# A fused state-read attention and top-2-of-4 mixture of experts: batch 5 in the dense form of batches 6 and 7, with new tables of the order

## The chip, the core and the metric

The kernel runs on one core of a Trainium2 chip, as one program with one launch. The metric is the device time of one execution in microseconds. The engines are TensorE (PE, matrix products; its weight loads are listed apart as PEld), VectorE (DVE), ScalarE (ACT), GpSimd (POOL) and SyncE (SP, which issues the DMAs here). Each engine works through its own list of instructions in order, and semaphores hold an instruction back until what it reads is there.

## What is computed

The first stage reads, per batch and head, a small state with attention in both directions. Its two results are joined, laid out as 544 tokens of 512 numbers per batch, and go through four attention experts, of which each token uses the two with the largest gate. Cut to what matters:

```python
# x (8, 8, 512, 64), state (8, 8, 32, 64): batch, head, token, width
a     = softmax(x @ state.T / 8)            # 512 x 32 per head
xread = a @ state
a2    = softmax(state @ x.T / 8)            # 32 x 512 per head
sread = a2 @ x
y = concat([xread, sread], axis=2)          # 544 tokens per head
y = y.transpose(0, 2, 1, 3).reshape(8, 544, 512)
logits = y @ w_gate                         # 4 experts, the largest 2 count
for e in range(4):
    q, k, v = y @ wq[e], y @ wk[e], y @ wv[e]            # 544 x 64 each
    att = softmax(causal(q @ k.T / 8))
    out += gate weight of e (0 if not chosen) * (att @ v @ wo[e])
```

wq and wk are scaled by 200, so the scores are large. The kernel therefore keeps every fp32 factor as a pair of fp16 numbers (a high half and the rest, the low half) and forms three products of each pair: high by high, high by low, low by high.

## The kernel before

**Work of a batch.** `front(b)` (from L557) loads x, splits it into halves `xh`, turns them into `xT`, forms the first scores and their softmax (`eb`, `mb`, `sbm`; its turned halves are `at`), multiplies the state by the weights (`gs`), and from `at` and `gs` gets the values `v`, the gate, the keys `kt` and the queries `qm`. For each of the four tiles of 128 tokens, `probs(b, unit)` (L920) forms the scores from `kt` and `qm`, adds the causal mask and takes the row maximum `mx` (a custom instruction on DVE), takes the exponential (ACT, tile `p`), splits it into halves `ph`, and turns these with one transposing DMA into `pt`. `reads(b, i)` (L964) multiplies `pt` by `v`, divides by the sum (`su`) and applies the gate (`c`), which gives `z`; its halves `zh` go through another transposing DMA. `result` (L1022) multiplies `z` by `wo_n` and writes the output `o`. `side(b, ...)` and `tail(g)` do the same for the 32 state rows of each batch, two batches at a time.

**Two forms.** A string of one letter per batch (`U` in `CFG`, L19) says how `units_of(b)` (L498) cuts the probabilities. Form S works with two slots: a slot is a query that is zero outside the expert that the token has chosen, so that two experts share one matmul of 128 rows. For it `front` forms Q token by token (24 matmuls of 256 columns), multiplies it by a mask (`qf`, mask `m`), splits it into `qh` and turns it by two transposing DMAs into `qm`. A read has 194 columns, for each of two slots. Form D ("dense") computes all four experts for all tokens, each with 64 rows, two side by side on the upper and lower half of the array. Q comes turned out of the product already (12 matmuls of 512 columns), with no mask and no DMA, and the gate is applied after the read, which has 65 columns for each of four experts. Its units are tile 1; the first two experts of tiles 0 and 2; their other two; and tile 3 in two halves:

```python
"S": [((0, "s"), (1, "s")), ((2, "s"),), ((3, "s"),)],
"D": [((1, "d"),), ((0, "0"), (2, "0")), ((0, "1"), (2, "1")), ((3, "0"),), ((3, "1"),)]
```

`all_experts(b)` (L506) names the tiles that are read densely, and `reads` and `front` branch on it.

**What sets the order.** Nothing is issued where it is written. Class `Steps` (L146 on) records each step with its engine or engines, what it reads and writes, and its buffers. `run` (L256) then plays three packed tables of numbers, `ORDER`: in which order the steps are issued, on which of the possible engines each goes, and which of the rotating buffers each gets. Every instruction is issued in one line there, L266, which is why the profile shows that line alone, and groups are told apart by their tiles:

```python
steps, ways, slots = (zlib.decompress(base64.b85decode(x)) for x in order)
...
for n in memoryview(steps).cast("H"):
    s = self.all[n]
    for f, kw in s["ways"][ways[n]][2]:
        f(**{k: v.ap() if isinstance(v, View) else v for k, v in kw.items()})
```

There are 2 buffers for `ph`, 3 for `pt`, 3 for `p`, and 8 banks of PSUM.

## Time and profile before

| | before |
|---|---|
| median of 3 runs | 278.22 us (277.75 to 279.74) |
| the profiled execution | 278.5 us, its span 276.7 us |
| granted TensorE clock | 1.00 |
| busy, share of the span: PE | 267.8 us, 97% |
| weight loads (beside PE) | 181.4 us, 66% |
| DVE | 248.6 us, 90% |
| ACT | 228.8 us, 83% |
| POOL | 173.9 us, 63% |
| chain that ended last | PE 71%, DVE 14%, ACT 7% |

The span is the time from the first to the last instruction of the profiled execution, and 1.8 us of its time lie around it. Busy shares are means over the whole span. What counts for a change is the stretch in which it lies and what is waited for there. A group of instructions of one form is shown with its count, its total busy time (overlaps counted once) and the mean length of one. Where matmuls overlap, the busy time over the count is less than the mean length, and it is what one of them costs.

### The profile page before, as it was taken

Reading aid. Unit: us, or ns where it says so; the run is one execution under the profiler, and the core shown is the slowest. Engines: PE = TensorE matmul, PEld = TensorE weight load, DVE = VectorE, ACT = ScalarE, POOL = GpSimd, SP = SyncE. Lnnn points to the kernel's source line nnn. Section 1 sums busy time; section 2 is a strip of 40 time slices with the busy share of each in tenths; the row PEclk is TensorE's granted clock in tenths of the full one; section 3 lists DMA queues with packets and bytes.
Section 4 is the critical chain, followed back from the end, with each engine's and each line's share of the span. In section 5 each row is a group of like instructions: output and inputs, shape, how many; then the busy total and the mean of one; then the engine's idle time right before and its main releaser. Section 6 shows DMA issues by size and latency. Waiting matters only on the chain.

```text
span 276.7 us, 9066 instructions
## 1 busy us (share of the span) xinstructions
PE 267.8 (97%) x3392; PEld 181.4 (66%) x3393; DVE 248.6 (90%) x743; ACT 228.8 (83%) x629; POOL 173.9 (63%) x250
## 2 busy tenths in 40 slices
PE   8989999899999999999999999999999999999995
PEld 4856756576477675666776757577477745486663
DVE  1699999999999999999999999998889989999862
ACT  4699999899899998998979888879668898778442
POOL 8852868497974898289859956687684661324000
PEclk9999999999999999999999999999999999999999
DMA  6985699999796999999999899996787988899994
GB/s 188 246 194 119 174 179 222 221 183 188 161 226 136 184 193 238 204 197 192 224 195 246 184 249 164 199 190 167 208 116 139 188 168 191 208 203 168 249 231 152
DMA packets 161804, 53.16 MB, mean 192 GB/s; under 512 B 140640, under 2 KB 157280, under 8 KB 161760
## 3 DMA queue, kind: packets, MB, share of 16 engines
q1 hardware_dynamic: 161760, 52.59, 95.1%
q8 instruction: 26, 0.43, 0.7%
q14 instruction: 18, 0.15, 0.2%
HBM read 11.02 MB, written 8.91 MB: 72 GB/s over the span
## 4 chain that ended last, share of the span: by engine, by line
PE 71%; DVE 14%; ACT 7%; issue 3%; POOL 2%; DMA 1%; DVEq 0%; POOLq 0%; ACTq 0%
PE bank L266 71%; DVE eb L266 2%; ACT p L266 2%; DVE sbm L266 1%; DVE qf L266 1%; DMA a2t<-a 1%; DVE xh L266 1%; DVE p L266 1%; ACT gs L266 1%; DVE gs L266 1%; DVE mb L266 1%; POOL eb L266 1%; ACT v L266 1%; ACT wn L266 1%; DVE m L266 1%
## 5 line engine op out<-in xcount | busy, mean ns | idle before, releaser
L266 PE MATMUL bank<-gs,at 128*128 128x260 f16 (+3 forms) x320 | 43.6, 284 | 0.7 <-ACT gs L266 0.7
L266 ACT ACTIVATE p<-p,mx 128x256 f32<-128x256 f32 (+3 forms) x80 | 41.8, 560 | 2.7 <-POOL mx L266 2.0
L266 PE MATMUL bank<-v,pt 128*128 128x194 f16 (+1 forms) x600 | 41.9, 226 | 0.5 <-DVE qf L266 0.4
L266 PE MATMUL bank<-kt,qm 64*128 64x128 f16 (+7 forms) x384 | 42.2, 299 | 0.0
L266 PEld LDWEIGHTS <-pt 128*128 128x128 f16 x600 | 38.7, 98 | 4.3 <-issue 1.3
L266 DVE CUSTOM_DVE_ANT_0 p<-bank,band 128x384 f32<-128x384 f32 (+3 forms) x80 | 35.9, 480 | 1.6 <-PE bank L266 1.3
L266 PEld LDWEIGHTS <-qm 64*128 64x128 f16 (+1 forms) x384 | 20.8, 95 | 18.4 <-issue 9.3
L266 PEld LDWEIGHTS <-at 128*128 128x128 f16 x288 | 27.7, 97 | 7.4 <-issue 1.1
L266 PE MATMUL bank<-at,gs 128*128 128x512 f16 (+1 forms) x116 | 29.9, 394 | 0.5 <-POOL at L266 0.5
L266 POOL TENSOR_TENSOR ph<-p,ph 128x1024 f16<-128x1024 f32 (+1 forms) x15 | 28.6, 1910 | 2.6 <-DVE ph L266 1.3
L266 PE MATMUL bank<-wo_n,z 128*128 128x512 f16 (+1 forms) x114 | 26.1, 368 | 0.0
L266 DVE SCALAR_TENSOR_TENSOR xh<-xn,xh 128x512 f16<-128x512 f32 x28 | 19.8, 723 | 1.7 <-POOL xh L266 1.5
L266 PE MATMUL bank<-wo_n,zp 128*128 128x512 f16 x84 | 20.3, 379 | 0.1
L266 ACT ACTIVATE o<-bank 128x512 f32<-128x512 f32 (+1 forms) x31 | 17.9, 582 | 2.9 <-PE bank L266 2.8
L266 ACT ACTIVATE z<-bank,c 128x64 f32<-128x64 f32 x78 | 17.4, 323 | 3.0 <-POOL c L266 2.8
L266 ACT ACTIVATE v<-bank 128x256 f16<-128x256 f32 x40 | 15.4, 394 | 3.9 <-PE bank L266 1.9
L266 PEld LDWEIGHTS <-z 128*128 128x128 f16 x114 | 10.7, 99 | 10.5 <-issue 0.9
L266 PEld LDWEIGHTS <-gs 128*128 128x128 f16 x108 | 10.3, 98 | 10.9 <-issue 0.9
L266 POOL TENSOR_TENSOR c<-su,wgt 128x6 f32<-128x6 f32 (+1 forms) x23 | 5.3, 235 | 17.8 <-DVE su L266 15.1
L266 ACT ACTIVATE ph<-p 128x768 f16<-128x768 f32 (+1 forms) x17 | 16.0, 944 | 0.2
L266 PEld LDWEIGHTS <-xh 128*128 128x128 f16 x416 | 14.1, 98 | 3.1 <-POOL xh L266 1.3
L266 POOL TENSOR_TENSOR qh<-qf,qh 128x768 f16<-128x768 f32 x8 | 14.3, 1786 | 2.6 <-ACT qh L266 2.0
(244 smaller groups left out, 674.9 us busy)
## 6 DMA issues: line engine op xcount, KB each, us to landing
out_dram<-o SPq DMA_DIRECT2D x33, 256.0 KB, 2.9
xn<-in_x_dram SPq DMA_DIRECT2D x14, 512.0 KB, 4.8
xn<-in_x_dram SPq DMA_DIRECT2D x4, 256.0 KB, 3.6
...
pt<-ph SPq DMA_TRANSPOSE x28, 4.1
...
```

Source lines behind the costliest of these rows:

```text
L266: f(**{k: v.ap() if isinstance(v, View) else v for k, v in kw.items()})
```

## The change

Batch 5 gets form D in place of form S, and the three tables are replaced by others that fit the new list of steps. The line of `CFG` and the first line of each table:

```diff
-           ... n_tpt=1, n_tz=1, n_pt=3, U="SSSSSSDD")
+           ... n_tpt=1, n_tz=1, n_pt=3, U="SSSSSDDD")
 ORDER = (
-        "c-jrs1A7o^7y!`M-@;nUTD7&cY;SGVP(v--wr$(CZQHhO+jjT<hx0rK0D*u(AQNPU2uKV?peSU4K*$Z=px_H7AtCrcHb@VikOPuJ2zWsl_(29J"
+        "c-jru1A7o^7y!`M-@@7!mR75^wQO#=p`n&-+qP}nwr$(CZM%Da#d(f5!~=r(V1OXt18E>3tOb9_3ArH&6ag<t3l4HXK1c)^pb)Hs^{@dvAt|H)"
...
```

The table is one line shorter, so that the line of all instructions is L265 in the changed kernel. In counts, batch 5 loses 24 matmuls of Q with 256 columns, 60 reads of 194 columns, and its masked queries with two DMAs; it gets 12 matmuls of Q with 512 columns and 120 reads of 65 columns, 8 more masked passes and as many more exponentials, and 20 transposes of 16 blocks for P in the whole kernel where there were 16 (10 of 12 blocks where there were 12). PE has 6493 rows in place of 6397, DVE 739 in place of 734.

The tables also move steps of other batches. From here on the rows are those of the two orders, with the numbers of tiles that tell buffers apart.

On PE, before, batch 5's first scores (those of tiles 0 and 1 together) follow 18 reads of batch 4, and begin with the form of 128 rows:

```order
L266 LDWEIGHTS pt_160
L266 MATMUL bank_84<-v_0_107,pt_160 128x194
L266 LDWEIGHTS qm_136
L266 MATMUL bank_82<-kt_137,qm_136 128x128
L266 LDWEIGHTS qm_136
L266 MATMUL bank_77<-kt_137,qm_136 128x128
L266 LDWEIGHTS qm_136
L266 MATMUL bank_82<-kt_137,qm_136 128x256
```

In the changed order, batch 5's first scores are those of tile 1 alone, 12 matmuls of 256 columns in the form of 64 rows, ahead of value products (`at`, `gs`):

```order
L265 MATMUL bank_83<-tv_0_110,tpt_202 64x259
L265 LDWEIGHTS qm_135
L265 MATMUL bank_80<-kt_139,qm_135 128x256
L265 LDWEIGHTS qm_135
L265 MATMUL bank_84<-kt_139,qm_135 128x256
...
L265 LDWEIGHTS at_122
L265 MATMUL bank_79<-gs_123,at_122 128x260
```

Where a dense read used to come only with batch 6, the first one (65 columns) now stands some 130 matmuls behind these scores, after the tail's products (`wn`, `xt_tail`) and six reads of 194 columns of batch 4:

```order
L265 LDWEIGHTS xt_tail_155
L265 MATMUL bank_82<-wn_75,xt_tail_155 64x132
L265 LDWEIGHTS pt_160
L265 MATMUL bank_84<-v_0_107,pt_160 128x194
...
L265 LDWEIGHTS pt_159
L265 MATMUL bank_83<-v_0_108,pt_159 128x65
```

On SP, which issues all transposes, before, the queries of batch 5 (`qm`) stand between batch 4's P and the outputs, and P of batch 5 comes in transposes of 12 and 16 blocks:

```order
L266 DMA_TRANSPOSE pt_160<-ph_157 128x12x128
L266 DMA_TRANSPOSE qm_136<-qh_142 128x12x128
L266 DMA_TRANSPOSE qm_136<-qh_143 128x12x128
L266 DMA out_dram<-o_179 128x512
L266 DMA_TRANSPOSE a2t_153<-a_0_154 128x8x128
L266 DMA_TRANSPOSE z_184<-zh_186 128x4x128
```

Changed, the two rows of `qm` are gone, and transposes of 16 blocks follow each other with outputs, a transpose of `z` and one of the state path (`a2t`) between them:

```order
L265 DMA_TRANSPOSE a2t_153<-a_0_154 128x8x128
L265 DMA_TRANSPOSE pt_160<-ph_158 128x16x128
L265 DMA out_dram<-o_180 128x512
L265 DMA_TRANSPOSE z_183<-zh_186 128x4x128
L265 DMA out_dram<-o_182 128x512
L265 DMA_TRANSPOSE a2t_153<-a_0_154 128x8x128
L265 DMA_TRANSPOSE pt_161<-ph_157 128x16x128
```

On DVE, at the program's start, before, two passes over the halves of x (`xh`) stand ahead of the first maximum of the softmax (`mb`):

```order
L266 TENSOR_SCALAR xh_95<-xn_87 128x512
L266 SCALAR_TENSOR_TENSOR xh_95<-xn_87,xh_95 128x512
L266 TENSOR_SCALAR xT_97<-bank_80 128x512
L266 TENSOR_REDUCE mb_118<-bank_84 128x16
L266 TENSOR_TENSOR eb_117<-bank_84,mb_118 128x512
```

Changed, there are four of them, and a second copy of `xT`:

```order
L265 TENSOR_SCALAR xT_97<-bank_80 128x512
L265 SCALAR_TENSOR_TENSOR xh_95<-xn_87,xh_95 128x512
L265 TENSOR_SCALAR xh_95<-xn_87 128x512
L265 SCALAR_TENSOR_TENSOR xh_95<-xn_87,xh_95 128x512
L265 SCALAR_TENSOR_TENSOR xh_94<-xn_90,xh_94 128x512
L265 TENSOR_SCALAR xT_97<-bank_82 128x512
L265 TENSOR_REDUCE mb_118<-bank_78 128x16
```

The first maximum has moved behind one more copy of `xT` and two more passes of `xh`.

## Rows read from the trace of the kernel before

**Rows 1.** Busy time by stretch: stretch, length, busy (instructions), clock, DMA share, GB/s.
```profile
40.00:60.00 20.00, 18.67 (x215) 12.30 (x214) 19.09 (x55) 18.92 (x54) 14.12 (x19) 1.00 1.01 198
...
180.00:240.00 60.00, 59.71 (x735) 38.52 (x732) 54.73 (x178) 48.13 (x132) 36.60 (x47) 1.00 0.86 176
```

**Rows 2.** Chain that ended last, three pieces: start us, length us, what.
```profile
120.84 85.44 PE bank L266 x1050
...
208.05 1.72 ACT p L266 x4
...
218.13 55.44 PE bank L266 x662
```

**Rows 3.** PE by form, scores: output<-inputs, shape, count, busy us, mean ns, idle before.
```profile
L266 PE MATMUL bank<-kt,qm 128*128 128x512 f16 x36 | 8.8, 380 | 0.0
...
L266 PE MATMUL bank<-kt,qm 64*128 64x512 f16 x60 | 8.3, 379 | 0.0
L266 PE MATMUL bank<-kt,qm 64*128 64x384 f16 x60 | 7.0, 325 | 0.0
L266 PE MATMUL bank<-kt,qm 128*128 128x384 f16 x36 | 6.9, 327 | 0.0
...
L266 PE MATMUL bank<-kt,qm 128*128 128x256 f16 x36 | 6.2, 273 | 0.0
...
L266 PE MATMUL bank<-kt,qm 64*128 64x128 f16 x60 | 6.0, 216 | 0.0
...
L266 PE MATMUL bank<-kt,qm 64*128 64x256 f16 x60 | 5.5, 272 | 0.0
L266 PE MATMUL bank<-kt,qm 128*128 128x128 f16 x36 | 5.0, 220 | 0.0
```

**Rows 4.** PE by form: reads, Q's two forms, and a product of the state path.
```profile
L266 PE MATMUL bank<-v,pt 128*128 128x194 f16 x360 | 33.4, 247 | 0.5 <-DVE qf L266 0.4
L266 PE MATMUL bank<-at,gs 128*128 128x512 f16 x108 | 26.1, 379 | 0.5 <-POOL at L266 0.5
...
L266 PE MATMUL bank<-gs,at 128*128 128x256 f16 x120 | 14.4, 272 | 0.7 <-ACT gs L266 0.7
...
L266 PE MATMUL bank<-v,pt 128*128 128x65 f16 x240 | 8.5, 194 | 0.0
...
L266 PE MATMUL bank<-wn,bd 64*32 64x512 f16 x168 | 5.9, 379 | 0.0
```

**Rows 5.** Timeline of PE: start us, length us, what, count.
```profile
222.28 0.88 PE L266 MATMUL bank<-wn,xt_tail 128*64 128x128 f16 x24
...
235.89 0.92 PE L266 MATMUL bank<-kt,qm 64*128 64x512 f16 x6
...
239.56 2.76 PE L266 MATMUL bank<-wo_n,zp 128*128 128x512 f16 x12
242.16 1.56 PE L266 MATMUL bank<-xt_tail,wn 128*128 128x64 f16 x48
...
244.22 1.63 PE L266 MATMUL bank<-v,pt 128*128 128x65 f16 x48
```

**Rows 6.** Timeline of SP's queue: the transpose of the probabilities of those scores.
```profile
242.09 1.58 SPq L266 DMA_TRANSPOSE pt<-ph  x1
```

**Rows 7.** Last lines of the views of tiles pt and zh, in this order.
```profile
DMA to landing us min/median/max: 3.2/4.1/6.5
...
DMA to landing us min/median/max: 2.4/3.4/5.7
```

**Rows 8.** The page's costliest groups: masked passes on DVE; POOL by form: low halves.
```profile
L266 DVE CUSTOM_DVE_ANT_0 p<-bank,band 128x384 f32<-128x384 f32 (+3 forms) x80 | 35.9, 480 | 1.6 <-PE bank L266 1.3
...
L266 POOL TENSOR_TENSOR ph<-p,ph 128x1024 f16<-128x1024 f32 x8 | 17.0, 2130 | 1.5 <-DVE ph L266 1.3 <-ACT ph L266 0.2
```

**Rows 9.** Tile xh: DVE's low halves, ns min/median/max, first and last start.
```profile
L266 DVE SCALAR_TENSOR_TENSOR xh<-xn,xh x28: 623/682/1642, 6.7 to 170.1; 128x512 f16<-128x512 f32 x28
```

**Rows 10.** The page's costliest groups: weight loads of the reads.
```profile
L266 PEld LDWEIGHTS <-pt 128*128 128x128 f16 x600 | 38.7, 98 | 4.3 <-issue 1.3
```

More of the change, by code (lines that the diff above doesn't have):

```diff
@@ L20 @@
            FRONT=1.5, FSPAN=1.0, TSPAN=1.3, TOFF=1.2, KT=3, p32=3, ph=2, at=1, et=1, gs=1, xh=4, a2=1, o=4, sn=1, qf=2,
[L21 removed]
+           n_eb=1, n_e2=1, n_a2t=1, n_xt_tail=2, n_z32=3, n_z=2, n_zh=2, n_tq=1, n_tv=2, n_tpt=1, n_tz=1, n_pt=3, U="SSSSSDDD")
 ORDER = (
     (
[L24 removed]
@@ new lines @@
+        "0GHqP+CF=(`|W@owPSYN3c14WyoI=fcGg1O8LOZttg=?ob5_cVx(u$E3v@A7QA^teyJE#%33t*;x>D|jz0lGw%-ykD7Hehgrj@hXcG)i3MGJRV"
+        "?XF$32p8$fxH!9S4{f}Cu(}#%6D-ONwNv)MqFszDZ=dY5#kzW0!S2}?8*U%1tQ%%uZKO@K(Kf~=+aw!dQ|ysFws8Ay*X@UmvX?r}BJ7oZv!C|M"
+        "Uh5lut5a>7O}7~~(`H#k`)#vrj?J}s_SBx)b1UcSYZ<F#aqgYYw-@$apICYK(jqOrRd5wuC0E&1wpaGoURxFSL94oWF2MfSKLhuFR~)-HR?Ss+"
+        "Q5N4Na0#6_Pp8gYBIo6jx*E>gRj~|~%tc#G_ttz}a+kuTbUx0xRL;Y_v-g(RrFQ-<iA(4FTzZ$rrFH)S)?}nA"
+    ),
+    (
+        "c-obfiw=b#3`05n|Bt?jqI6?$k(j8w)^07dW{vz4IzBW#D^+Z~n{Tr<Adq{ZKUc5fsxqRQPrRQO9O3=$0QNm6r*!~?7_o82KhE&D<AaWR43Ow`"
+        "P8cnGx1P+vYJ)`HqeJXdeo8UPxok6*iPBOg+M@#)g&gFFI10F!C>DcTy+Q=a1YaeSR6M3~%lPSx0L#3xt5f6x&Se$}Eescf$;`z3-rj9Ng&0@X"
+        "#_$~v6*;@QN`xw-stl*X?#$LIQ}f!96pc^bS{trnRTVPWg8z9WpRdnRjOqXKAba>GQ%>lz6PMdfe&eV*PBj*5AMD$;H!dc^0rmrh5CJ&"
+    ),
@@ new lines @@
+    (
+        "c-m!?2W|sF3<K5m{~w2=bqWyMNNx*7iq!4QW@ejZTAJBf>oM%#$D_^7)4a#3$8)v3o%Zn3cU$mD2krHzMy&-n{Sj1%NC7QEM54E=M5zdugmC_="
+        "ZWc%8W3eLEZcjqWp1vF!wLcQ)fTDqDR4|5(Qei6!Scqp$OBDeY<vf?b_p=VmDz|OjV^1a1=}>~|SS07La{%C4H7!g9eIDuv3VJ+I2b{2Uq~W7H"
+        "?_Xm1E}fFn*PyQ8sP0}Y%49;m?Vu!z=K~f*x}!A2pb{d|PII1!+mmzt$U|F|tjkvfsNnLM^)&2{nooyHErxK;XeA~)d?62JhD!?WIbrxaI7M@u"
+        "ykZL7Qho;BP%~u6nJL+fLio!~>IdH#sK&8)Qz@#Kv!=z*YEMWmY2m&*#1MGKah7X}vF;51lbEm2i>{!~Gcg-OU;k|vL(~oY&~3uV(D{w3JoL}@"
+        "vBN>i%udsYl-w}gt210FBQ+ZIgA0I{YDM&VYgp0l>S;Cj3Owt&v-e89SK)i`?B+JU0A-K{b^"
```

74 lines of the change are left out of this document (30 added, 44 removed).

## The prediction

> **What bounds the kernel now.** I read the busy time by stretch first, then the chain of work that ended last, then the groups of matmuls by form, and at last the single places on TensorE (PE) and on the DMA queue that the change touches.
>
> The busy times by stretch show two regimes [rows 1]. In 40 to 60 us, DVE and ACT are each busy for 19 of 20 us and PE has 1.33 us of holes. In 180 to 240 us, where batch 5's probabilities and reads lie, PE is busy 59.71 of 60, DVE 54.73, ACT 48.13, POOL 36.60. The chain says the same [rows 2]: from 120.84 us on it is PE for 85.44 us without a break, then a detour of 11.9 us that starts with ACT's exponentials p and runs over the other elementwise engines, and from 218.13 us PE again for 55.44 us. So PE work that is taken out of batch 5 shortens the time, as long as what feeds PE keeps up; DVE, at 91% of that stretch, is the next in line.
>
> **The change part by part.** Batch 5 goes from form "S" to form "D". The work of the other batches stays; their order, engines and buffers come from new tables.
>
> *Scores.* In the S form a tile has 6 matmuls over all 128 rows (slot against slot, two experts at a time) and 6 over 64 rows. In the D form all 12 are of 64 rows, and two such run side by side on the two halves of the array. So six matmuls of each width (128 to 512 columns) move from the 128-row groups to the 64-row ones. By the groups of [rows 3], busy time over count, one costs 244 ns against 138 ns at 512 columns, 192 against 117 at 384, 172 against 92 at 256, 139 against 100 at 128. The sum is 6 x (106 + 75 + 80 + 39) = 1.80 us less.
>
> *Reads (probabilities times V).* 60 matmuls of 194 columns go, 120 of 65 columns come. At 33.4/360 = 92.8 and 8.5/240 = 35.4 ns [rows 4] this is 5.57 us less and 4.25 us more: 1.32 us less.
>
> *Q.* 24 matmuls of 256 columns (14.4/120 = 120 ns) go, 12 of 512 (26.1/108 = 242 ns) come [rows 4]: 2.88 against 2.90 us, nothing. What goes beside them, the masked copy qf, its halves and two transposing DMAs of 12 blocks, was off PE's path.
>
> PE's sum is thus -3.10 us. The busy times of groups overlap a little at their seams, so I keep -2.5 to -3.3.
>
> *Other engines.* DVE gets 8 more masked passes, 8 x 480 ns = 3.8 us [rows 8], and loses four qf, one qh and three low-half passes of 768 columns; between nothing and 3.8 us I take +1.3. ACT gets 8 more exponentials and loses 16 copies of z and some of qf's halves; it has 12 us to spare in the stretch [rows 1], so I leave it at nothing. POOL gets three more low-half passes of 1024 columns, 3 x 2.13 = 6.4 us [rows 8], and a few low halves of z, and loses qh and small steps: about +6 us. SP has four more 16-block transposes of P, two of 12 blocks fewer, and two fewer for Q: as many issues as before. In the 60 us stretch this makes DVE about 56, POOL 43 and PE 56.6, in a stretch that should shrink to 56.9. The work that hides the extra DVE time is PE's own, and the cover is nearly used up.
>
> *The start.* The new order puts two more xh conversions ahead of the first softmax on DVE (the order rows show it). That pulls about 2 us of DVE work out of the DVE-bound stretch and can hold up PE's first transposes. Bounds: a gain of the 1.33 us of holes in 40 to 60 us [rows 1], a loss of one conversion, 0.7 us [rows 9]. I take 0.
>
> *New waits.* In D form a tile's read hangs on its own scores through mask, exponential, two halves and a transposing DMA. The fastest of this kind in the trace are the scores at 235.89 us of 0.92 us, whose transpose is issued at 242.09 [rows 5, 6]: 5.3 us, to which the landing adds 3.2, 4.1 or 6.5 us (min, median, max) [rows 7], so 8.5, 9.4 or 11.8 us. In the changed order, the first dense read of batch 5 (tile 1) stands behind its scores by this PE work: 12 result matmuls 2.76 us, 6 more half of that [rows 5], 18 reads of 194 columns 1.67 and 12 gate and V products about 1.44 [rows 4], 6 scores of 384 columns and 6 of 128, 1.30 [rows 3], 48 narrow matmuls of the state path at 5.9/168 = 35 ns, 1.69 [rows 4], and the tail's 24 at 0.88 us [rows 5]. That is 11.1 us, and about 10 after the seams of some ten groups (a group's end overlaps the next, as 239.56 + 2.76 against 242.16 [rows 5], by 0.1 us or a little more). Against 9.4 us at the median the read just makes it; against 11.8 it waits 1.8 us. Queued behind the waiting read are all matmuls of PE; what is late next is the z of tile 1. Its result stands 18 reads, 12 result matmuls, 12 scores and 24 matmuls of the state path later, between 5 and 6 us by the same rows, of which the transposing DMA of z alone takes 2.4, 3.4 or 5.7 us [rows 7]: up to 2 us again. A third place, the reads of tile 3, is wider in the new order and should pass. I take 0.4 us for each of the first two and 0.2 for the rest, 1.0 us; bounds 0 and 3.
>
> *Sum.* The profiled execution took 278.5 us (span 276.7 and 1.8 around it), 0.3 above the median of 278.22. 278.5 - 3.1 + 0 + 1.0 = 276.4 us, 0.65% under the median.
>
> [...] The loads of P last 98 ns each [rows 10]. Yet the 48 matmuls of 65 columns at 244.22 us, each with a load of its own, are through in 1.63 us [rows 5], and 48 x 98 ns would be 4.7: the loads overlap, and do not set the pace. [...]
>
> DVE's conversions xh take 623 ns at best and 1642 at worst [rows 9] with one and the same shape, so something can stretch a DVE pass by a microsecond; the median of 682 says that it is rare. [...]
>
> **The rivals.** (A) *The whole saving arrives and the start gives a little.* For it: PE stood still for only 0.29 us of the 60 [rows 1], so its feeders were early, and 1.33 us of holes in 40 to 60 us are there to be won. Against: the 10 us place. Without new waits and with half of the start's gain: 278.5 - 3.1 - 0.7 = 274.7 us.
>
> (B) *DVE takes PE's place as the bound.* DVE's busiest share where it sets the pace is 19.09 of 20, 95.5% [rows 1]. Batch 5's 56 us of DVE work at that share needs 58.6 us instead of 60: only 1.4 us are won, and with 1.0 of waits the time is 278.1 us, no change. For it: the detour in the chain runs over these engines [rows 2]. Against: PE's waits there are short, 0.29 us in 60.
>
> (C) *POOL holds up DVE.* Three more POOL passes of 2.13 us [rows 8] that each block DVE for their length add 6.4 us to DVE's 56: 62.4 us, at 95.5% 65.3 us for the stretch of 60, so +5.3 at worst; with half of that 59.2/0.955 = 62.0, +2.0. In between, +3.5: 282.0 us, slower. It decides once DVE's work in the stretch passes 57.3 us (60 x 0.955), that is, from 1.3 us of blocking on. Against: the median in [rows 9] stays near the minimum beside a POOL that is busy 36.60 of 60.
>
> (D) *Loads set the pace of reads*: 60 more at 98 ns [rows 10] = +5.9 in place of -1.32, so 278.5 - 1.8 + 5.9 + 1.0 = 283.6 us. Nearly ruled out by the 1.63 us for 48 [rows 5].
>
> **How the numbers follow.** A measurement of this kernel can tell about 1% from no change: under 275.4 is faster, over 281.0 slower. Forecast (most of the saving, some of it eaten, 275.4 to 278): 0.48. A: 0.33, all under 275.4. B: 0.08, within 1%. C: 0.09 and D 0.01, slower; 0.01 for waits at both places at their bounds with the start's loss (278.5 - 2.5 + 0.7 + 4.4 = 281.1). So faster 0.33, same 0.56, slower 0.11. The range: low 274.0, A with all the start's gain and the larger PE sum (278.5 - 3.3 - 1.3 = 273.9); high 279.5, the forecast with the smaller PE sum, the start's loss and waits of 3 us less a little (278.5 - 2.5 + 0.7 + 3.0 = 279.7). What is left out is C, D and little of A, about 0.2.
>
> **What the new profile would show.** Scores: the 128-row groups with 30 matmuls each at the same means, the 64-row ones with 66. Reads: 360 of 65 columns near 35 ns each. PE's busy total about 264.7 us. New waits: idle of PE ahead of the reads of 65 columns near 200 us, released by the DMA of pt, and ahead of a result, released by that of z. B: DVE above 95% in 180 to 240 us. C: means of DVE's passes longer by tens of nanoseconds there, or ph, mx and c waiting for POOL. The prediction is wrong if PE's busy total does not fall by about 3 us, or if PE stands still for more than 3 us after 75 us.

## The result and the profile after

The changed kernel takes 282.51 us (median of 4 runs, 281.25 to 282.98) against 278.03 us for the kernel before on the same chip. The ratio is 1.0143, 95% interval 1.0098 to 1.0188: 1.4% slower, where 0.65% faster was forecast and 279.5 was the upper end of the range. The profiled execution has a span of 280.8 us, 4.1 more than before, at a granted clock of 1.00 as before.

The page of the changed kernel, its busy times (part 1) and the chain that ended last by engine (part 4):

```profile
PE 266.9 (95%) x3441; PEld 177.4 (63%) x3441; DVE 253.0 (90%) x748; ACT 227.3 (81%) x627; POOL 180.6 (64%) x251
...
PE 58%; DVE 16%; ACT 10%; DMA 7%; POOL 5%; issue 3%; SPq 0%; DVEq 0%; POOLq 0%; ACTq 0%
```

TensorE's share of the chain fell from 71% to 58%: more of the span now hangs on what feeds it. Its work did fall. TensorE by form, changed kernel (shape, count, busy us, mean ns, idle before), to be set beside [rows 3, 4]:

```profile
L265 PE MATMUL bank<-at,gs 128*128 128x512 f16 x120 | 28.9, 379 | 0.5 <-DVE v L265 0.5
L265 PE MATMUL bank<-v,pt 128*128 128x194 f16 x300 | 27.9, 247 | 0.4 <-ACT v L265 0.3
...
L265 PE MATMUL bank<-v,pt 128*128 128x65 f16 x360 | 13.2, 194 | 0.5 <-DMA pt<-ph 0.5
L265 PE MATMUL bank<-gs,at 128*128 128x256 f16 x96 | 11.5, 272 | 1.6 <-DVE z L265 1.6
```

The reads went from 33.4 + 8.5 to 27.9 + 13.2 us, the two forms of Q from 26.1 + 14.4 to 28.9 + 11.5, and the eight forms of scores together from 53.7 to 51.7: -0.8, -0.1 and -2.0, that is 2.9 us less. The busy total fell only by 0.9 (267.8 to 266.9): the groups overlapped one another less, by 42.6 instead of 44.5 us (the sum over all forms less the busy total). The time went elsewhere. Two matmul groups stand at the same place of the program in both kernels, the tail's 24 products of 128 columns and reads of batch 2. Timeline of TensorE (start us, length us), the kernel before and then the changed one:

```profile
69.05 0.88 PE L266 MATMUL bank<-wn,xt_tail 128*64 128x128 f16 x24
...
137.65 1.59 PE L266 MATMUL bank<-v,pt 128*128 128x194 f16 x17
```

```profile
69.32 0.88 PE L265 MATMUL bank<-wn,xt_tail 128*64 128x128 f16 x24
...
140.70 1.50 PE L265 MATMUL bank<-v,pt 128*128 128x194 f16 x16
```

With the spans of 276.7 and 280.8 us this cuts the loss in three:

| stretch | before | after | difference |
|---|---|---|---|
| A: to the tail's product | 69.05 | 69.32 | +0.27 |
| B: from there to the reads of batch 2 | 68.60 | 71.38 | +2.78 |
| C: from there to the end, with all of batch 5 but its load | 139.05 | 140.1 | +1.05 |

So about 3 us are lost before any step of the dense form runs: the new tables alone do that. Busy time by stretch (columns as in [rows 1]) of the changed kernel, and of the kernel before for the stretches that are not in [rows 1]; the last line of each is C:

```profile
40.00:60.00 20.00, 19.65 (x230) 12.98 (x228) 19.55 (x56) 18.78 (x54) 12.36 (x16) 1.00 1.01 196
180.00:240.00 60.00, 57.62 (x762) 35.02 (x760) 56.46 (x186) 51.76 (x135) 44.53 (x52) 1.00 0.91 188
180.00:225.00 45.00, 43.15 (x609) 27.28 (x608) 42.97 (x138) 38.37 (x106) 32.58 (x39) 1.00 0.88 177
75.00:140.70 65.70, 63.28 (x801) 43.98 (x801) 64.40 (x182) 57.11 (x166) 47.23 (x56) 1.00 1.07 193
140.70:280.79 140.09, 134.56 (x1748) 86.47 (x1745) 124.29 (x406) 106.91 (x296) 81.03 (x95) 1.00 0.95 195
```

```profile
75.00:137.65 62.65, 62.47 (x800) 43.62 (x799) 60.70 (x175) 58.20 (x168) 46.89 (x55) 1.00 1.08 199
180.00:225.00 45.00, 44.71 (x588) 30.74 (x586) 41.59 (x134) 35.81 (x105) 31.45 (x39) 1.00 0.81 160
137.65:276.69 139.04, 135.61 (x1700) 90.65 (x1697) 123.12 (x403) 105.67 (x297) 72.90 (x96) 1.00 0.94 191
```

TensorE's holes went from 62.65 - 62.47 = 0.18 to 65.70 - 63.28 = 2.42 us in B from 75 us on, from 0.29 to 2.38 us in 180 to 240 us, and from 139.04 - 135.61 = 3.43 to 140.09 - 134.56 = 5.53 us in all of C. So 2.10 us of C's loss is TensorE standing still. The rest is overlap: 2.9 us of its work by form went out, and its busy time in C fell by only 1.05, so 1.85 us of overlap between groups was lost. DVE is busy 64.40 of 65.70 us in B from 75 us on (98%; it was 97% before), and 42.97 of 45 (95.5%) in 180 to 225 us. Time for which a step of DVE is held counts as busy in these rows (the gate step of 2.13 us that is shown below stands in B's). Where TensorE waits, and for whom (timeline of the changed kernel; the wait stands in brackets):

```profile
92.37 2.14 PE L265 MATMUL bank<-gs,at 128*128 128x256 f16 x18 [1.60 <-DVE z L265]
...
190.34 1.47 PE L265 MATMUL bank<-wo_n,z 128*128 128x512 f16 x6 [0.48 <-DMA z<-zh]
192.38 0.83 PE L265 MATMUL bank<-kt,qm 64*128 64x384 f16 x12 [0.57 <-DVE z L265]
201.56 1.46 PE L265 MATMUL bank<-at,gs 128*128 128x512 f16 x6 [0.52 <-DVE v L265]
...
227.61 0.91 PE L265 MATMUL bank<-v,pt 128*128 128x65 f16 x24 [0.53 <-DMA pt<-ph]
```

One large wait stands in B and a few of half a microsecond in C. What makes the large one is on DVE and POOL. Timelines of DVE, and then of POOL, at the gate of batch 2; first the kernel before:

```profile
87.63 0.32 DVE L266 SCALAR_TENSOR_TENSOR gt<-gt,gt 128x20 f32<-128x20 f32 x1 [0.30 <-ACT gt L266]
87.88 0.54 DVE L266 TENSOR_TENSOR z<-bank,c 128x384 f32<-128x384 f32 x1
88.34 0.28 DVE L266 SCALAR_TENSOR_TENSOR bd<-bank,bd 128x128 f16<-128x128 f32 x1
...
89.77 0.28 DVE L266 TENSOR_TENSOR wgt<-gt,gs 128x20 f32<-128x20 f32 x1
```

```profile
87.88 2.13 POOL L266 TENSOR_TENSOR ph<-p,ph 128x1024 f16<-128x1024 f32 x1
```

And the changed kernel:

```profile
88.74 2.13 DVE L265 SCALAR_TENSOR_TENSOR gt<-gt,gt 128x20 f32<-128x20 f32 x1
```

```profile
88.70 2.13 POOL L265 TENSOR_TENSOR ph<-p,ph 128x1024 f16<-128x1024 f32 x1
```

A gate step on 20 columns that takes 0.32 us stands for 2.13 us, as long as the POOL pass that began 0.04 us ahead of it, and ends within 0.04 us of it. In the kernel before, the same step began 0.25 us ahead of the pass, and what DVE did beside the pass read a bank of PSUM, reduced a row or was a short reciprocal (0.17 to 0.54 us each); the next step with two inputs from SBUF, `wgt`, came 0.24 us before the pass ended, and took 0.28 us. The POOL pass is that of batch 1 and stands in both kernels.

There is a second such place, in C, at the gate of batch 5; timelines of DVE and POOL in the changed kernel:

```profile
186.42 1.61 DVE L265 SCALAR_TENSOR_TENSOR gt<-gt,gt 128x16 f32<-128x16 f32 x1
```

```profile
186.35 1.64 POOL L265 TENSOR_TENSOR ph<-p,ph 128x768 f16<-128x768 f32 x1
```

This POOL pass is one of batch 4. Where the step isn't held it takes 0.23 to 0.26 us (kernels 11, 12, 14, 15 and 17 below).

### The profile page after: what moved, and what is told of

Same layout as the page of the kernel before. It is cut to its first block, busy times and chain, and to the rows that moved or that the text cites. A ratio compares the mean times of both kernels' runs of the same rounds, so it can differ in the third digit from the quotient of the medians.

```text
span 280.8 us, 9174 instructions
## 1 busy us (share of the span) xinstructions
PE 266.9 (95%) x3441; PEld 177.4 (63%) x3441; DVE 253.0 (90%) x748; ACT 227.3 (81%) x627; POOL 180.6 (64%) x251
## 4 chain that ended last, share of the span: by engine, by line
PE 58%; DVE 16%; ACT 10%; DMA 7%; POOL 5%; issue 3%; SPq 0%; DVEq 0%; POOLq 0%; ACTq 0%
PE bank L265 58%; DMA a2t<-a 4%; DVE xh L265 2%; DMA pt<-ph 2%; ACT p L265 2%; DVE eb L265 1%; DVE sbm L265 1%; DMA xn<-in_x_dram 1%; POOL ph L265 1%; POOL eb L265 1%; DVE a L265 1%; ACT v L265 1%; DVE et L265 1%; ACT kt L265 1%; POOL at L265 1%
## 5 line engine op out<-in xcount | busy, mean ns | idle before, releaser
L265 ACT ACTIVATE p<-p,mx 128x256 f32<-128x256 f32 (+3 forms) x88 | 45.9, 557 | 3.1 <-POOL mx L265 2.3
L265 PE MATMUL bank<-gs,at 128*128 128x260 f16 (+3 forms) x296 | 40.7, 285 | 1.7 <-DVE z L265 1.6
L265 PE MATMUL bank<-v,pt 128*128 128x65 f16 (+1 forms) x660 | 40.8, 218 | 0.9 <-DMA pt<-ph 0.5
L265 PE MATMUL bank<-kt,qm 64*128 64x128 f16 (+7 forms) x384 | 40.5, 298 | 0.8 <-DVE z L265 0.6
L265 PEld LDWEIGHTS <-pt 128*128 128x128 f16 x660 | 37.7, 98 | 5.7 <-issue 2.3
L265 POOL TENSOR_TENSOR ph<-p,ph 128x1024 f16<-128x1024 f32 (+1 forms) x19 | 38.4, 2021 | 3.8 <-ACT tlg L265 1.3
L265 DVE CUSTOM_DVE_ANT_0 p<-bank,band 128x384 f32<-128x384 f32 (+3 forms) x88 | 39.4, 480 | 1.0 <-PE bank L265 0.6
L265 PE MATMUL bank<-at,gs 128*128 128x512 f16 (+1 forms) x128 | 32.7, 393 | 0.5 <-DVE v L265 0.5
L265 PEld LDWEIGHTS <-qm 64*128 64x128 f16 (+1 forms) x384 | 19.8, 95 | 18.0 <-issue 8.0
L265 PEld LDWEIGHTS <-at 128*128 128x128 f16 x264 | 25.1, 97 | 9.2 <-issue 2.1
L265 PE MATMUL bank<-wo_n,z 128*128 128x512 f16 (+1 forms) x114 | 26.1, 368 | 1.1 <-DMA z<-zh 0.5
L265 DVE SCALAR_TENSOR_TENSOR xh<-xn,xh 128x512 f16<-128x512 f32 x28 | 21.3, 778 | 1.5 <-ACT xh L265 0.9
L265 PE MATMUL bank<-wo_n,zp 128*128 128x512 f16 x84 | 20.1, 380 | 0.0
L265 ACT ACTIVATE ph<-p 128x1024 f16<-128x1024 f32 (+1 forms) x20 | 19.7, 983 | 0.2
L265 PEld LDWEIGHTS <-gs 128*128 128x128 f16 x120 | 11.4, 98 | 12.2 <-issue 1.2
L265 ACT ACTIVATE o<-bank 128x512 f32<-128x512 f32 (+1 forms) x30 | 16.9, 575 | 1.8 <-PE bank L265 1.2
L265 PEld LDWEIGHTS <-z 128*128 128x128 f16 x114 | 10.6, 98 | 12.0 <-issue 1.9
L265 POOL TENSOR_TENSOR at<-et,at 128x512 f16<-128x512 f32 x10 | 12.7, 1274 | 6.0 <-DVE cmp L265 4.2
L265 PEld LDWEIGHTS <-xh 128*128 128x128 f16 x416 | 14.1, 98 | 3.9 <-DVE xh L265 1.4
L265 ACT ACTIVATE v<-bank 128x256 f16<-128x256 f32 x40 | 15.4, 403 | 1.3 <-PE bank L265 0.8
L265 ACT ACTIVATE gs<-bank 128x260 f16<-128x260 f32 (+3 forms) x33 | 15.7, 491 | 0.6 <-PE bank L265 0.5
L265 ACT ACTIVATE z<-bank,c 128x64 f32<-128x64 f32 x62 | 13.9, 331 | 2.6 <-POOL c L265 1.6
```

## The experiments

Each kernel below was timed against the kernel before on its own chip. The rows show one profiled execution each, cut into the same three stretches; "old start" is the kernel before up to the middle of the program (780 steps), "new start" the changed one, and the ends likewise.

| kernel | A | B | C | span | ratio to before (interval) |
|---|---|---|---|---|---|
| before | 69.05 | 68.60 | 139.05 | 276.7 | 1 |
| changed | 69.32 | 71.38 | 140.10 | 280.8 | 1.0143 (1.0098 to 1.0188) |
| 1 old start, dense end | 68.84 | 68.67 | 141.29 | 278.8 | 1.0073 (1.0049 to 1.0097) |
| 2 new start, old end | 69.99 | 71.30 | 139.21 | 280.5 | 1.0124 (1.0092 to 1.0156) |
| 3 DVE and POOL forms alone | | | | | none: it computes nothing of the reference |
| 4 before, gate step late | 68.79 | 69.68 | 139.03 | 277.5 | 1.0051 (1.0033 to 1.0069) |
| 5 changed, gate product on POOL | 69.86 | 72.46 | 140.18 | 282.5 | 1.0178 (1.0137 to 1.0220) |
| 6 changed, pass behind the mask | 69.84 | 74.26 | 140.40 | 284.5 | 1.0237 (1.0206 to 1.0268) |
| 7 changed, pass shortened | 69.77 | 70.33 | 139.80 | 279.9 | 1.0160 (1.0110 to 1.0210) |
| 8 changed, transposition earlier | 69.72 | 70.92 | 139.96 | 280.6 | 1.0118 (1.0089 to 1.0147) |
| 9 both of 7 and 8 | 71.12 | 69.83 | 139.65 | 280.6 | 1.0097 (1.0069 to 1.0126) |
| 10 changed, gate ahead of the pass | 70.47 | 71.78 | 140.25 | 282.5 | 1.0209 (1.0187 to 1.0232) |
| 11 as 1, one pass of batch 4 on DVE | 68.92 | 68.60 | 140.88 | 278.4 | 1.0035 (1.0014 to 1.0056) |
| 12 as 11, last pass of batch 5 on DVE | 68.88 | 68.44 | 141.38 | 278.7 | 1.0107 (1.0091 to 1.0124) |
| 13 as 1, POOL's passes shortened | 68.88 | 68.40 | 139.92 | 277.2 | 1.0057 (1.0036 to 1.0077) |
| 14 as 1, DVE's passes shortened | 68.92 | 68.46 | 139.82 | 277.2 | 1.0009 (0.9994 to 1.0024) |
| 15 as 1, all five shortened | 69.09 | 68.60 | 139.71 | 277.4 | 0.9999 (0.9982 to 1.0016) |
| 16 as 1, DVE's passes on POOL | 68.58 | 68.54 | 142.58 | 279.7 | 1.0100 (1.0073 to 1.0127) |
| 17 changed, 7, 8 and 14 together | 71.11 | 69.12 | 138.87 | 279.1 | 1.0073 (1.0049 to 1.0098) |
| 18 as 10, with the edit of 11 | 69.76 | 71.58 | 140.66 | 282.0 | 1.0165 (1.0145 to 1.0185) |

The orders are packed tables, so an edit of an order is shown as the steps it moves, with their engine.

### 1 and 2: start and end apart

```diff
 steps 0 to 779    -changed order   +order of the kernel before     (1)
 steps 780 on       changed order, batch 5 dense
```

> The changed kernel with the first 780 of its 1883 steps (of batches 0 to 4, all of them work that both kernels have) in the order, on the engines and in the buffers of the kernel before; the rest, with batch 5 in dense form, as changed. The same step of PE (the reads of batch 2's tile 2) starts at 137.65 us before and at 140.70 us changed, so 3.05 us of the loss lie ahead of it and 1.05 us behind it. Theory S (the losses are local: the start's new order costs 3.05 us by itself): 278.0 + 1.05 = 279.1 us, 278.5 to 279.8. Rival (the loss at the start is made good or made up for later, so that only the dense batch counts): 282 us and more. Second rival (the dense end is a gain once the start is mended): under 277 us.

```diff
 steps 0 to 779     changed order
 steps 780 on      -changed order   +order of the kernel before, batch 5 with slots     (2)
```

> The reverse: the kernel before, batch 5 in slots, with its first 780 steps in the order, engines and buffers of the changed kernel. No step of batch 5's dense form is in it. Theory S: 278.0 + 3.05 = 281.1 us, 280.3 to 281.8. Rival (the loss comes from the dense batch alone): 278.0 us.

The dense end behind the old start loses 2.0 us by the ratio (C is 141.29 against 139.05), the new start with batch 5 as before 3.4 us (A and B are 3.64 longer, C 0.16). Either part alone makes the kernel slower, and the start, which has nothing of batch 5 but its load, the more so. Together they lose less than their sum: C is 140.10 behind the new start and 141.29 behind the old one, perhaps since the other engines have a lead behind a late start; no run shows that.

### 3: which DVE steps a POOL pass holds

DVE runs 100 steps on 20 columns of fp32, once for each form, while POOL makes 8 low-half passes of 1024 columns; one stretch has DVE alone, and one lets 40 small POOL steps run beside 8 two-input passes of DVE.

> None of the computation, the output is zero: six phases, in each of which POOL and DVE run beside each other on tiles of their own. POOL subtracts 128x1024 eight times, while DVE does 100 operations of 20 columns: of two SBUF inputs, of one SBUF input, of one PSUM and one SBUF input, a reduction; then eight DVE subtractions of 128x1024 beside 40 POOL operations of two columns; then the two-input operations alone. Theory L: with two SBUF inputs the longest takes about as long as a POOL pass, 2.1 us, and one in each of the eight passes is that long; with one input, or with a PSUM input, none is over 0.3 us; beside DVE's subtractions POOL's small operations take 1 us and more now and then. Rival (the long products had another cause, a semaphore or the memory): all phases alike.

Views of the tiles (ns min/median/max, first and last start): two inputs from SBUF, one input from SBUF, one from PSUM and one from SBUF, a reduction; last, POOL's small steps beside DVE's passes.

```profile
L52 DVE SCALAR_TENSOR_TENSOR d_two<-sm,sn x100: 171/179/2125, 3.3 to 39.0; 128x20 f32<-128x20 f32 x100
```

```profile
L54 DVE TENSOR_SCALAR d_one<-sm x100: 169/176/2118, 39.4 to 74.8; 128x20 f32<-128x20 f32 x100
```

```profile
L56 DVE SCALAR_TENSOR_TENSOR d_psum<-bank,sn x100: 171/178/178, 75.2 to 96.2; 128x20 f32<-128x20 f32 x100
```

```profile
L58 DVE TENSOR_REDUCE d_red<-sm x100: 167/174/174, 96.6 to 117.2; 128x1 f32<-128x20 f32 x100
```

```profile
L43 POOL TENSOR_SCALAR m_big<-src x40: 191/192/1221, 117.7 to 136.4; 128x2 f32<-128x2 f32 x40
```

A step of DVE with two inputs from SBUF, or a tensor-scalar step with one, stood here for up to a whole POOL pass (2125 and 2118 ns for 179 and 176; the passes took 2119 to 2157); of 100 steps that read PSUM, and of 100 reductions, none did (maxima 178 and 174). The expectation missed for one input: it had nothing over 0.3 us there. It went the other way too: POOL's steps of 192 ns stood up to 1221 ns, the length of a DVE pass (1225). In kernel 8 the step that was first to start went free: gt began 0.06 us ahead of the pass and took 0.18 us.

### 4: the hold alone, in the kernel before

```diff
-DVE gt<-gt,gt      (gate of batch 2)
 DVE z<-bank,c
+DVE gt<-gt,gt
```

> The kernel before, batch 5 untouched, with one step of DVE moved: the gate pass of batch 2 that ran at 87.63 us for 0.32 us goes behind the next DVE step (the reads' product of 0.54 us), so that it meets the POOL pass that starts at 87.88. Theory S: the gate pass is held until about 90.0 (some 1.8 us) and the time rises by 1 to 2 us, ratio 1.004 to 1.007: the new start's loss made without the change. Rival N: held or not, the time stays within 0.5 us (ratio below 1.002), and the new start loses by something else.

Timelines of DVE, POOL and TensorE in this kernel:

```profile
87.45 1.91 DVE L262 SCALAR_TENSOR_TENSOR gt<-gt,gt 128x20 f32<-128x20 f32 x1
```

```profile
87.20 2.13 POOL L262 TENSOR_TENSOR ph<-p,ph 128x1024 f16<-128x1024 f32 x1
```

```profile
90.61 2.12 PE L262 MATMUL bank<-gs,at 128*128 128x256 f16 x18 [0.96 <-DVE v L262]
```

One step moved by one place costs 1.4 us (B is 1.08 longer), with nothing else changed. The hold is a cause; it isn't yet shown to be the only one.

### 5, 6 and 10: moving a step out of the way

```diff
-DVE  wgt<-gs,gt    (gate of batch 2)      (5)
+POOL wgt<-gs,gt
```

> The changed kernel with one step on another engine: the last product of batch 2's gate (wgt from gt and gs, 128x20) on POOL in place of DVE. POOL's low-half pass of 1024 columns for batch 1, which started at 88.70 us, then stands behind the gate in POOL's list and cannot start ahead of the gate's product gt on DVE, which started at 88.74 us and took 2.13 us instead of 0.17. Theory L (POOL's pass held DVE's operation of two SBUF inputs, and this delay of 1.96 us is on the path): 2.0 us less than the changed kernel, 1.3 to 2.7: 280.5 us; the gate's product back at about 0.2 us. Rival (DVE is simply full there, the long product is only where it shows): 282.5 us, within 0.5.

```diff
-POOL ph<-p,ph      (low half, batch 1, tile 3)     (6)
 POOL m<-wgt        (mask of batch 2)
+POOL ph<-p,ph
```

> The changed kernel with one step moved in POOL's list: the low-half pass of 1024 columns of batch 1's tile 3 now stands behind the mask m of batch 2, which waits for the whole gate of batch 2. In the kernel with the gate's product on POOL the pass had only been moved from the gate's gt (back at 0.2 us) to the next operation of two SBUF inputs, wgt<-wgt, 1.91 us. Here it can meet neither. Theory L (POOL's pass holds DVE's two-input operation for as long as it runs, and DVE is on the path there): 1.5 to 2.7 us less than the changed kernel, which is 3.5 to 5 us above before; so 1.0 to 3.0 us above before. Rival (DVE full, the hold is no loss): as the changed kernel, 3.5 to 5 us above before.

```diff
+DVE a<-a,e,s       (batch 3)              (10)
-DVE xh<-xh,xn      (batch 4)
 DVE gt, v
-DVE a<-a,e,s
 DVE gt, gt<-gt,gt, c<-su,wgt, sbm, xt_tail, gs, z<-bank,c, v<-bank,v
+DVE xh<-xh,xn
 and on SP the transposition of a one place ahead, that of xh two places back
```

> The changed kernel, nothing left out, four steps moved at 86 to 92 us: on DVE the product a of batch 3 goes ahead of the conversion xh of batch 4, and that conversion goes behind the four steps that read a PSUM bank or reduce, so that the gate pass gt and the small product c come 0.7 us earlier, ahead of POOL's low-half pass, and only steps that this pass does not hold stand beside it; on SP the transposition of a goes one place ahead and that of xh two places back. Theory Q (order against the pass and the transposition are the start's cause): no step of DVE is held at 88 to 91 us, TensorE waits for neither z nor a, about 2 of the 3 us come back: ratio 1.005 to 1.009. Rival N (DVE is full there, lateness only moves on): the held time shows up at another step or TensorE waits elsewhere, ratio 1.012 or more.

None of the three is faster than the changed kernel, against what was expected: 6 and 10 are slower, and 5, at 1.0 us more by the ratio, isn't clear of noise. In each the gate step gt was free and another step was held: in 5 a gate product `wgt` at 91.68 us by the pass at 91.61, in 6 `twg` and then a mask `m` (1.87 and 1.57 us at 94.72 and 96.61, beside three POOL passes in a row). B of 5 and 6 also holds some microseconds at a lower granted clock (last section): in 5 the 48 products of `a2t` took 2.71 us where the changed kernel's took 1.57. In 10 the moved step fell 0.03 us behind the start of the pass; timelines of DVE and POOL:

```profile
89.67 0.18 DVE L262 SCALAR_TENSOR_TENSOR gt<-gt,gt 128x20 f32<-128x20 f32 x1
89.76 2.12 DVE L262 TENSOR_TENSOR c<-su,wgt 128x6 f32<-128x6 f32 x1
```

```profile
89.73 2.13 POOL L262 TENSOR_TENSOR ph<-p,ph 128x1024 f16<-128x1024 f32 x1
```

The two are tied: the DVE step ahead of `c` and the POOL step ahead of the pass both waited for `su` from ACT here (0.38 and 3.42 us), so `c` and the pass come out together although `c` was moved. Kernel 18, 10 with the edit of 11 below, has the same B (71.58) and is 1.2 us better than 10.

> The same four moves, and batch 4's third tile with its low half on DVE in place of POOL (the edit that took 0.65 us off the dense end behind the old start, by ending the hold of its gate pass). Nothing left out. If the two cures add: ratio 1.002 to 1.006, still above the kernel before, since the dense end keeps its waits for DVE. If not: the same as the run beside it.

### 7, 8 and 9: taking the pass away, and what then is late

In 7 the pass is cut to 128 columns and the order stays; 7/8 of that half are left out.

```diff
-        split(n, ph[:, :n], ph[:, n:2 * n], p32[:, :n])
+        short = 128 if b == 1 and unit[0][0] == 3 else None     # low half only
+        split(n, ph[:, :n], ph[:, n:2 * n], p32[:, :n], short)
```

> The changed kernel with one pass shortened: the low half of the probabilities of batch 1's fourth tile, the POOL pass of 1024 columns that ran from 88.70 to 90.83 us in the changed kernel, handles 128 columns (the other 7/8 of that half are left out; its buffer takes the other of two slots). The order is untouched. Theory S (the held gate is the price of the new start): the one-column-group gate pass on DVE falls from 2.13 back to about 0.3 us, the wait of 1.6 us that TensorE has at 92 us goes, the span falls by about 1.8 and the ratio to before from 1.014 to about 1.008. Rival N (DVE is full there and the hold only shows where its lateness lands): the gate pass is short, but TensorE waits for the same sum a little later, span within 0.6 of 280.8, ratio 1.012 or more.

The gate step takes 0.42 us, and B is 1.05 us shorter, but the time hardly moves (281.95 us, 0.6 under the changed kernel; its ratio rests on an execution of 284.75 too). TensorE's timeline shows why:

```profile
92.64 0.97 PE L262 MATMUL bank<-wn,bd 64*32 64x512 f16 x24
95.30 0.87 PE L262 MATMUL bank<-a2t,xh 128*128 128x64 f16 x24 [1.69 <-DMA a2t<-a]
```

It comes 1.8 us earlier to the state product (94.44 in the changed kernel) and then waits 1.69 us for a transposition of `a`. In the kernel before, SP issues that transposition at 87.21 us, one transposition of `xT` behind the `z` ones; in the new order two of `xT` and a load of `xn` stand ahead of it, and it is issued at 89.95 in the changed kernel and at 90.48 in 7. (The tile `a` that it reads is done later as well, at 88.42 us in the changed kernel instead of 87.18.) Kernel 8 moves only it; kernel 9 does both.

```diff
 SP xT<-xh   (batch 4)
+SP a2t<-a   (batch 3)                    (8, 9)
 SP xT<-xh
-SP a2t<-a
```

> The changed kernel whole, with only that transposition issued one place earlier on SP. Theory Q: the gate hold still binds, so nothing is won: ratio 1.012 to 1.016. If the transposition alone were the cause, 1.007.

> As s_pool_start_short (batch 1's fourth tile's low half shortened to 128 columns on POOL, the rest of it left out), and on SP the transposition of a for batch 3 issued before the second transposition of x instead of behind it. Theory Q (gate hold and late transposition stand in parallel; whichever is left costs about 2 us): TensorE's wait of 1.7 us at 95 us goes, the side step of batch 3 starts at about 93.6 instead of 95.3, ratio 1.006 to 1.010. Rival N (DVE is full there, every cure moves the lateness on): a third wait takes its place, ratio 1.013 or more.

Kernel 8 left the step gt unheld by chance, since gt began 0.06 us ahead of the pass, and the next small step took the hold; timeline of DVE:

```profile
88.66 0.18 DVE L262 SCALAR_TENSOR_TENSOR gt<-gt,gt 128x20 f32<-128x20 f32 x1
88.75 2.12 DVE L262 TENSOR_TENSOR c<-su,wgt 128x6 f32<-128x6 f32 x1
```

B is 70.92, little better than 71.38. With both (9) B is 69.83 and the ratio 1.0097; in kernel 17, which has the same edits there, B is 69.12 against 68.60 in the kernel before. From the tail's product to the product of `a2t` it is 23.74 us before, 26.15 in the changed kernel, 25.53 in 7, 25.69 in 8, 25.04 in 9 and 23.81 in 17. So hold and transposition are two latenesses side by side, and most of the loss of B goes only when both go; each B here is that of one execution. Between 9 and 17, which are alike there, the transposition's landing seems to decide: issued at 89.99 and 89.56, the product behind it starts at 96.16 and 94.92, and the longest landing of that tile is 6.0 and 4.6 us. (In 9 the trace puts the wait down to a mask `m` that had just ended; in 17 the product ran before that mask.)

What is left is A. With the old start it is 68.58 to 69.09 us in nine profiles, with the new one 69.32 to 71.12 in ten. In the first 27 us TensorE waits 0.9 us for `sn` and 1.3 for `xh` in the changed kernel, 1.1 for `xh` and 0.4 for `lg` in the kernel before. In 9 and 17 some 1.3 us of it lie in the first 13 us: 8 transpositions of `xn` took 1.91 us and the 32 products with `et` 4.4, against 1.16 and 3.8 in the changed kernel's profile, at a granted clock of 1.00 in each. Why these executions ran slower there was not settled.

### 11 to 16: what the dense end waits for

The waits of TensorE in kernel 1 from 178 to 228 us (waited for, us in total, times, longest):

```profile
PE bank L262 <- DMA pt<-ph: 1.0, 1, 1.0
PE bank L262 <- DMA z<-zh: 0.9, 1, 0.9
PE bank L262 <- DVE qm L262: 0.6, 1, 0.6
PE bank L262 <- DVE v L262: 0.5, 1, 0.5
```

```diff
-POOL ph<-p,ph   (low half, batch 4, tile 2)      (11)
+DVE  ph<-p,ph
```

> The first kernel of this call (start of before, changed end), with the low half of batch 4's tile 2 on DVE in place of POOL (0.95 us more on DVE, 1.64 less on POOL). In the changed kernel this pass ran on POOL from 186.35 us and the gate's product gt of batch 5 on DVE from 186.42 us took 1.61 us instead of 0.16. Theory L: the product back at 0.16 us; DVE wins 1.44 and pays 0.95, so 0 to 1 us less than the first kernel. Rival (the end is bound by the amount of DVE's work): 0.5 to 1 us more than the first kernel.

```diff
-POOL ph<-p,ph   (last low half, batch 5, tile 3; on top of 11)      (12)
+DVE  ph<-p,ph
```

> Start of before, changed end, batch 4's tile 2 low half on DVE (the kernel that was 1.25 us above before), and also the low half of the second half of batch 5's tile 3 on DVE in place of POOL, where it took 2.15 us from 218.13 and where PE then waited 1.1 us for the transposed probabilities of that tile. Theory J (the dense reads of batch 5 stand just in time, and POOL's slow low halves make them late): this wait goes, 0.5 to 1.1 us less than that kernel: 0.2 to 0.8 us above before. Rival B (DVE is the bound in that stretch): DVE pays 1.22 us more, so 0 to 1 us more than that kernel.

In 11 the hold of a gate step at 183 us (1.4 us) goes and the time falls by 1.1 us. In 12 the wait for `pt` before tile 3's reads goes as well, and the time rises by 2.0 us by the ratio (C by 0.5, but this profiled execution is the fastest of the four): DVE has one pass of 1.2 us more, and TensorE waits 1.31 us for DVE's `xt_tail` at 219.56 instead. Then the low-half passes of batch 5 were cut to 128 columns (7/8 of them left out), POOL's three (13), DVE's two (14), all five (15), by the lines shown for 7 with other units.

> Start of before, changed end (the kernel that was 1.9 us above before), with POOL's three low-half passes of batch 5 cut from 1024 to 128 columns: seven eighths of these low halves are left out. POOL wins 5.6 us and what it holds. Theory P (POOL's added passes are what takes the gain back): 2 to 4 us less, below before. Theory J with other causes (DVE's amount of work, DMA landing, the order): 0 to 1 us less.

> The old start with the dense end (ratio 1.0073 earlier), its two low-half passes of batch 5 that DVE makes (1024 columns, 1.2 us each) shortened to 128 columns; 7/8 of those halves are left out. Theory D (DVE is what the dense end waits for): about 2 us of DVE work gone before the tiles 1 and 0 of batch 5, the waits at 186 to 196 us shrink, span down by 1 to 2 us, ratio 1.000 to 1.004. Rival L (what TensorE waits for is the length of each tile's chain, exponential, split, transposing DMA, not an engine that is full): the first read's wait shrinks by at most 1 us since its own split is shorter, the others stay; span down by 0.3 to 0.8, ratio 1.005 to 1.006. Rival P (POOL's passes): no change, 1.007.

> The old start with the dense end, all five low-half passes of batch 5 (two on DVE, three on POOL) shortened to 128 columns; 7/8 of those halves are left out. If the split passes are what eats the saving, by engine time or by the chain's length, most of the 4.7 us of added waits go and the time falls below the kernel before: 275 to 277, ratio 0.990 to 0.997. If the passes are not it and the order of the other steps is late as it stands, the ratio stays at 1.003 or above (the sum of the 0.5 us that POOL's three gave and of the DVE's two).

POOL's three passes, 4.1 us of POOL's time (2.3 instead of 6.4), are worth 0.45 us by the ratio, give or take 0.9, so not clear of nothing; DVE's two, 1.9 us of DVE's time (0.66 instead of 2.53), are worth 1.8. (C is alike in 13 and 14 because the profiled execution of 13 is its fastest, 278.96 us, and that of 14 its slowest, 279.0.) Busy times of 180 to 225 us in kernel 1, and then in kernel 14 (the third pair is DVE, the last POOL):

```profile
180.00:225.00 45.00, 42.30 (x615) 26.80 (x612) 41.46 (x133) 37.34 (x102) 34.19 (x40) 1.00 0.81 167
```

```profile
180.00:225.00 45.00, 43.52 (x642) 27.87 (x640) 39.89 (x138) 38.77 (x105) 32.98 (x40) 1.00 0.88 180
```

With DVE at 39.89 us instead of 41.46, TensorE gets 1.2 us more done in the same 45. But 14 changes two things. Its gate step of batch 5 starts 0.16 us ahead of POOL's pass of batch 4 (183.04 us), and isn't held; timeline of DVE:

```profile
182.88 0.23 DVE L262 SCALAR_TENSOR_TENSOR gt<-gt,gt 128x16 f32<-128x16 f32 x1
```

In kernels 1 and 13 it stands 1.61 us, and 11 puts the end of this hold at 1.1 us. Beyond 11, kernel 14 is worth some 0.7 us (1.0009 against 1.0035), and that is all that is left for DVE's two passes themselves. In 16 the same two passes go to POOL, with nothing left out.

> The old start with the dense end (ratio 1.0073), the two low-half passes of batch 5 that DVE makes put on POOL at the same places; nothing is left out. Theory D (DVE is full): 2.4 us of DVE time gone, but POOL needs 2.1 us for a pass that DVE makes in 1.2, and its passes hold small DVE steps: the first read of batch 5 comes some 1 us later, the rest earlier; ratio 1.002 to 1.006. Rival L (the length of the chain to the transposition): 1.008 to 1.012, since both chains grow by about 1 us.

The time is 0.8 us above kernel 1, which isn't clear of noise. DVE is hardly relieved: it is busy 41.02 us in 180 to 225, against 41.46 in kernel 1 and 39.89 in 14, because the moved pass (POOL, 179.51 us, 2.13 long) now holds the step ahead of it in the same gate, and gt itself stands 1.66 us again at 183.66. Timelines of DVE and of TensorE:

```profile
179.54 2.14 DVE L262 TENSOR_TENSOR gt<-lg,gs 128x16 f32<-128x16 f32 x1
```

```profile
207.27 3.27 PE L262 MATMUL bank<-v,pt 128*128 128x194 f16 x60 [1.11 <-DVE qm L262]
```

TensorE waits 1.11 us for `qm`, where kernel 1 waits 0.6. So POOL is no way out, but 16 doesn't tell the holds from the 0.9 us by which POOL's passes lengthen the tiles' chains. Whether 14 gains beyond the hold by DVE's time or by the shorter chains, these runs don't tell apart either. Even with all five passes cut and the gate step free (15) the time only equals the kernel before: C is 139.71 against 139.05, so 2.9 + 0.66 = 3.6 us of the saving are still eaten. The named waits of TensorE from 178 to 228 us in 15 (for `v`, `qm`, `tq`, `a2t`) are 0.3 to 0.5 us each and 1.5 us together; the rest was not followed. Which part the new order makes, and which the dense form, stays open; a kernel with the old order of all other steps and a dense batch 5 was not built.

### 17: do the parts add

> The changed kernel with the three suspected costs taken away: POOL's pass of batch 1 and DVE's two low-half passes of batch 5 shortened to 128 columns (7/8 of these halves left out), the transposition of a one place earlier. If start and end add up as the separate runs say (start 2 us of its 3 back, end 1.8 us back): 1.0143 less 0.0070 less 0.0064, so 0.999 to 1.004. If they don't add (one cure's gain is taken by the other's stretch), 1.008 or more.

1.0073, between the two expectations. B and C behave as they should (69.12, and 138.87, under the 139.05 of before); what is missing is A at 71.11. No version tried is faster than the kernel before.

## Why the prediction was wrong, step by step

**PE's sum: right by form, wrong for the span.** Forecast -3.1 (bounds 2.5 to 3.3), measured -2.9: scores -2.0 for -1.80, reads -0.8 for -1.32, Q -0.1 for nothing. The reads were mis-sized a little: 65 columns cost 36.7 ns each (13.2/360) instead of 35.4. The loads did not set the pace, as the 48 reads in 1.63 us had said [rows 5]; rival D is out. The step that failed is the next one, from the groups to TensorE's time: "the busy times of groups overlap a little at their seams" allowed 0.6 us, and 1.85 us of overlap went in C. PE's busy total is 266.9, not 264.7. Why the groups overlap less was not followed.

**The start: wrong, +3.05 instead of 0 (bounds -1.33 to +0.7).** This is half of the miss. The step that failed took the two conversions `xh` for all that the new order does before batch 5, and bounded it by the holes of one stretch. In that stretch it was even right: TensorE's holes in 40 to 60 us went from 1.33 to 0.35 us. The loss is 30 us later, at a place that was not looked at, by a gate step held by POOL (2.13 instead of 0.32 us) and a transposition issued a queue place too late (4, 7, 9), with up to some 2 us in the first 69 us in other executions.

**New waits: 2.10 instead of 1.0 (bounds 0 to 3), and mostly at other places.** The size is inside its bounds; the places are not those named. The first dense read has no named wait, nor has tile 1's result. The 0.48 us at 190.34 are an earlier tile's result that waits for its z, and the 0.57 at 192.38 are scores that wait until DVE has read tile 1's z out of its bank. Tile 3's read, which "should pass", waits 0.53 in the changed kernel and 0.95 in kernel 1. What the step did not count is the second hold, 1.61 us at the gate of batch 5, whose end is worth 1.1 us in 11, as much as the whole difference between 2.10 and 1.0. (The 4.4 us of waits in the prediction's sum of 281.1 aren't derived there: the two places at their bounds give 1.8 + 2 = 3.8.)

**Other engines: right in time, wrong in price.** DVE was put at about 56 us and POOL at 43 in the 60 us; they are 56.46 and 44.53. "The cover is nearly used up" was written, and the price set to nothing all the same. What a microsecond of DVE costs there the runs don't give as one number: 12 added 1.2 us and lost 2.0 by the ratio, 11 took 1.4 of hold off, put 0.95 of work on and won 1.1.

**Rival B** (278.1 us) named an engine that half of the named waits of C fall to, but its sign, DVE above 95% in 180 to 240 us, did not come: it is 56.46 of 60, 94%. Kernel 1 is 280.8 us by its median, so B was under-priced as well.

**Rival C** (282.0 us, 0.09) came out at almost the measured time for a partly right reason, and so partly by luck. The hold is real (3, 4, 11). That each POOL pass blocks DVE for its length was C's assumption, and no run shows it of the three passes: in kernel 3 eight passes, 17.2 us in all, made 100 two-input steps 14.6 us longer (32.5 us, and 17.9 with POOL idle), but no step that read PSUM or reduced (178 and 174 ns at most). And C tied it to batch 5's three new POOL passes, which cost 0.45 us within noise (13), and to the 57.3 us of DVE work. What decided, beside a late transposition, are two old passes, of batch 1 and batch 4, and two steps of 20 and 16 columns; the first hold lies in B, where C looked for nothing. The argument against it failed: the median of `xh` [rows 9] says how often a long DVE pass is held (one of the 28 took over 0.9 us: 1642 ns at 48.74 us, beside a POOL pass of 1633 at 48.20), not where a short one on the critical chain meets a POOL pass. The mean of the gate step by form went from 203 to 803 ns at 20 columns, and from 158 to 457 at 16, rows that were never read.

**The signs.** Both signs that the prediction gave for its being wrong came true: PE's busy total fell by 0.9 us, not by about 3, and its holes after 75 us went from 0.18 + 3.43 = 3.61 to 2.42 + 5.53 = 7.95 us, 4.3 more.

**The sum.** 276.4 + 3.05 (start) + 1.1 (standing still) + 1.85 (lost overlap) + 0.2 (TensorE by form) = 282.6 us, the span of 280.8 and 1.8 around it. The start is shown by experiments (2, 4, 7 to 9, 17), the second hold by 11; the lost overlap is measured and its cause is open.
